# A fused attention and gated feed-forward kernel: tile 3 of batch 0 moved into tile 1's gates, three tiles of batch 1 transposed by DMA, numerators and loads of batches 2 and 3 rescheduled

## The chip, the cores and the metric

The kernel runs on one core of one Trainium2 chip. The metric is device time in microseconds (us), and lower is better. Besides the timed runs there is one profiled execution, of which the trace holds the start and the length of every instruction and every DMA packet. The engines are named as the profile names them: PE is TensorE (PEld its weight loads), DVE is VectorE, ACT is ScalarE, POOL is GpSimd and SP is SyncE, which in this kernel only issues DMAs.

## The reference: what is computed

A linear attention ("cosFormer") over 8 batches, 8 heads, 576 positions and a head size of 64 is followed by a gated feed-forward layer with RMS normalization. All inputs and outputs are float32.

```python
def phi(x, c, s):                       # c, s: cos and sin of pi/2 * pos / S
    r = np.maximum(x, 0.0)
    return np.concatenate([r * c, r * s], axis=-1)      # 128 features
q_p, k_p = phi(q, cos_w, sin_w), phi(k, cos_w, sin_w)
kv  = np.einsum('bhsf,bhsd->bhfd', k_p, v)
z   = np.sum(k_p, axis=2)
num = np.einsum('bhsf,bhfd->bhsd', q_p, kv)
den = np.einsum('bhsf,bhf->bhs', q_p, z)[..., None] + 1e-06
x   = (num / den).transpose(0, 2, 1, 3).reshape(B * S, H * D)   # 4608 x 512
xn  = x / sqrt(mean(x * x) + 1e-6) * rms_g
g   = xn @ w_gate                                       # 512 -> 1536
out = (silu(g) * (xn @ w_val)) @ w_out                  # 1536 -> 512
```

## The kernel before, in words

**Tiles and blocks.** The 576 positions of a batch are split into four tiles of 128 (j = 0 to 3) and a tail of 64. Two tails make one tail tile of 128 rows, so there are four of those. The feed-forward layer works on blocks of 512 rows: blocks 0 to 7 are the four tiles of batches 0 to 7, and block 8 is the four tail tiles. Blocks are worked in the order 0, 1, 2, 3, 4, 5, 6, 8, 7.

**The steps of one tile.** `q_phi` makes the features of q (tile `qp`) on DVE and ACT, a transposition turns them (`q_tr_pe` on PE or `q_tr_dma` by DMA) into `qpT`. `nd_pe` (L418; matmuls at L421) multiplies them with the batch's key-value product and gives numerators and denominators of eight heads in the one PSUM tile `psA`. `nd_post` (L479) reads `psA` on DVE: an addition (L461), a reciprocal (L464) and a product (L471), which leaves the tile's x in SBUF. `x_sq` (L483) takes the mean square on ACT and the power -1/2 on POOL; `x_norm` (L495, DVE L499) gives the normalized tile `xn` in bf16. The next `nd_pe` can write `psA` only when the product L471 of the one before has read it.

**The transposition of a normalized tile.** The gate and value matmuls need the tile transposed in `xnT`. On PE this is `x_tr_pe` (four 128x128 transpositions, L518) into a PSUM bank, and `x_tr_evac` (L520) copies the bank to `xnT` on ACT or DVE. By DMA it is `x_tr_dma` (L511, one instruction on SP's queue, L512).

**The key-value product.** `k_phi` makes key features, `v_cast` casts v, and `kvz_pe` sums over positions into `psA`. A batch's k, v and q are loaded to tiles `raw`, of which there are five in a ring (`load_kv`, `load_q`); `load_q_tails` loads the tails of two batches. Batches up to 2 have k and v in one layout, batches from 3 on in a "wide" layout (`wide(b)`), whose load is one DMA of 112 rows and one or two small ones. Loads go through SP's queue or through POOL's.

**One feed-forward block.** For each of 12 chunks n, `gval_mm` (L528) makes four gate matmuls into `psG[n % 2]` and four value matmuls into `psV[n % 2]`; `gval_h` takes the SiLU on ACT (L547) and the product on DVE (L548) into `hT`. Two banks of each kind alternate. Then `out_step` (L551) makes 12 matmuls for each of four output tiles into `psC[j % 2]`, and `out_store` copies and stores them.

**The order is written by hand.** The schedule is manual: each engine runs its instructions in the order of the program and waits by semaphores. `at(blk, n, where, f, ...)` puts a call in a slot of a block: `gval_step` runs the slot's "pe" list, then the matmuls of chunk n, then the "pre" list, then SiLU and product, then the "post" list. Slots 12 to 15 are the four output steps, which have a "mid" as well. `out_first` is the output of block 0: 48 matmuls in the order of its list `todo`, 12 of them to a slot, with slots 12 to 15 around them.

**Block 0 starts by hand.** Before the slots there is straight-line code (L578 to L709) for batch 0. Its first chunks are worked in units: `units[i] = (j0, j1, n0, n1)` are the tiles and chunks of unit i. Units 0 to 3 are one tile wide (tiles 0, 1, 0, 1; chunks 0 to 3, then 4 to 7), units 4 to 7 are tiles 2 and 3 together with two chunks each. `unit_mm(i, wg)` writes `psG[i % 2]`, `unit_mm(i, wv)` writes `psV[i % 2]`, `unit_silu(i)` and `unit_h(i)` follow. `filler(n, bank)` is n matmuls of zeros. The core of what the change touches there reads:

```python
    unit_mm(3, wg)                 # tile 1, chunks 4-7
    x_tr_pe(0, 3, psC[0])          # tile 3 transposed
    x_tr_evac(V, 0, 3, psC[0])
    unit_silu(3)
    unit_h(1)
    unit_mm(4, wg)                 # tiles 2 and 3, chunks 0-1
    for i in range(2, 4):
        unit_mm(i, wv)
        unit_h(i)
    unit_silu(4)
```

**Batch 1 and batch 2 around the change.** The list `X1` (L744) places the four tiles of batch 1 within `out_first`: `nd_pe`, `nd_post` and `x_sq` of tile j at the first place, `x_norm` at the second, the transposition on PE (`x_tr`) at the third. Batch 2's tiles have `nd_pe` in chunks 6, 8, 10 and 12 of block 1 and `x_norm` with `x_tr_dma` one slot later. Batch 2's q is loaded by POOL's queue in slot 11 of block 0, batch 3's k, v and q by SP's queue in slots 0, 5 and 8 of block 1.

Of the kernel before, what the change touches and what calls it, by code (L numbers as in the profile page):

```python
# [17 lines left out]
def kernel(  # L18
# [11 lines left out]
    nc = tc.nc  # L30
    B, H, S, D = q.shape
    DM = H * D
    DFF = moe_w_gate.shape[1]
    P = 128
    TB = 512
    HP = H // 2
# [4 lines left out]
    NDT = DM // P  # L41
# [5 lines left out]
    V, A, G = nc.vector, nc.scalar, nc.gpsimd  # L47
# [10 lines left out]
    psG = [ps.tile([P, 512], FP32, name=f"psG{i}") for i in range(2)]  # L58
    psV = [ps.tile([P, 512], FP32, name=f"psV{i}") for i in range(2)]
    psC = [ps.tile([P, 512], FP32, name=f"psC{i}") for i in range(2)]  # L60
# [13 lines left out]
    def wide(b):  # L74
        return b > 2
# [4 lines left out]
    def kv_rows5(src, b, r0, r1):  # L80
        part = src[b, :, 0 : NC5 * (KP - 1), :].rearrange(
            "h (p c) d -> p h (c d)", c=NC5
        )[r0 : min(r1, KP - 1)]
        return bass.AP(part.tensor, part.offset, [[NC5 * D, r1 - r0]] + list(part.ap)[1:])
# [6 lines left out]
    def raw_tile(which, b):  # L91
        if (which, b) not in raw:
            t = ring.tile([P, H * NC5 * D], FP32, name="raw", tag="raw")
            raw[(which, b)] = t
        return raw[(which, b)]

    def raw_kv(which, b):
        t = raw_tile(which, b)
        if wide(b):
            return t[:, :].rearrange("p (h e) -> p h e", h=H)  # L100
        return t[:, 0 : HP * NC * D].rearrange("p (hp e) -> p hp e", hp=HP)
# [4 lines left out]
    def load_kv(which, b, hps=(0, HP), eng=nc.sync):  # L106
        src = k if which == "k" else v
        if not wide(b):
            return eng.dma_start(
                out=raw_kv(which, b)[:, hps[0] : hps[1], :], in_=kv_rows(src, b, hps)  # L110
            )
        last = KP if b < B - 1 else KP - 1
        for r0, r1 in ((0, KM), (KM, last)):
            eng.dma_start(out=raw_kv(which, b)[r0:r1, :, :], in_=kv_rows5(src, b, r0, r1))
        if last < KP:
            eng.dma_start(
                out=raw_kv(which, b)[last:KP, :, :].rearrange("p h (c d) -> p h c d", d=D),
                in_=src[b, :, S - 1 : S, :].rearrange("h s d -> s h d").unsqueeze(2)
                .to_broadcast([1, H, NC5, D]),
            )  # L120
# [19 lines left out]
    for c0, c1 in ((0, 4), (4, NC)):  # L140
        nc.sync.dma_start(
            out=raw_kv("k", 0)[:, :, c0 * D : c1 * D],
            in_=kv_rows(k, 0, (0, HP))[:, :, c0 * D : c1 * D],
# [24 lines left out]
    wg = one.tile([P, NDT, DFF], BF16, name="wg")  # L168
    wv = one.tile([P, NDT, DFF], BF16, name="wv")
# [42 lines left out]
    part, left = [], 1e-6  # L212
# [8 lines left out]
    def g_spread(bank, t):  # L221
# [12 lines left out]
        out=th[:, 0:NTAB], in0=fidx[:, :], scalar1=S - 1.0, scalar2=ang,  # L234
        op0=ALU.min, op1=ALU.mult,
    )
    for c0, c1, less in ((0, 9, 576.0), (13, 14, 64.0)):
        V.tensor_scalar(
            out=th[64:128, c0:c1], in0=fidx[64:128, c0:c1], scalar1=-less, scalar2=ang,
# [3 lines left out]
        out=th[:, NTAB : 2 * NTAB], in0=th[:, 0:NTAB], scalar1=math.pi / 2.0,  # L243
# [4 lines left out]
        out=sel[:, :, :], in_=ident[0:4, 0:4].unsqueeze(2).to_broadcast([4, NDT, P])  # L248
# [17 lines left out]
    xnT = [one.tile([P, NDT, TB], BF16, name=f"xnT{i}") for i in range(2)]  # L266
# [212 lines left out]
    def nd_post(b, j):  # L479
        nd_rec(b, j)  # L480
        nd_div(b, j)
# [38 lines left out]
    def x_tr_evac(eng, b, j, bank, ts=(0, NDT)):  # L520
        dst = bank.bitcast(BF16).rearrange("p (t s) -> p t s", s=P)
        copy(eng, x_dst(b, j)[:, ts[0] : ts[1], :], dst[:, ts[0] : ts[1], :])
# [48 lines left out]
    def filler(n, bank):  # L571
        for _ in range(n):
            nc.tensor.matmul(
                bank[:, :], lhsT=warm[:, 0:P], rhs=warm[:, :], start=True, stop=True
            )
# [30 lines left out]
    units = [(j, j + 1, 4 * i, 4 * i + 4) for i in range(2) for j in range(2)]  # L606
    units += [(2, 4, n, n + 2) for n in range(0, 8, 2)]
    sg_of = {}

    def unit_mm(i, w, by_rows=False):  # L610
        j0, j1, n0, n1 = units[i]
        bank = (psG if w is wg else psV)[i % 2]
        width = (j1 - j0) * P
        todo = [(n, t) for n in range(n0, n1) for t in range(NDT)]
        if by_rows:
            todo = [(n, t) for t in range(NDT) for n in range(n0, n1)]
        for n, t in todo:
            nc.tensor.matmul(  # L618
                bank[:, (n - n0) * width : (n - n0 + 1) * width],
                lhsT=w[:, t, n * P : (n + 1) * P],  # L620
                rhs=xnT[0][:, t, j0 * P : j1 * P],
                start=(t == 0 and (n == n0 or not by_rows)),
                stop=(t == NDT - 1 and (n == n1 - 1 or not by_rows)),
                skip_group_check=by_rows,
            )

    def unit_silu(i):
        sg_of[i] = four.tile([P, TB], FP32, name="sg", tag="sg")
        A.activation(out=sg_of[i][:, :], in_=psG[i % 2][:, 0:TB], func=AF.Silu)

    def unit_h(i):
        j0, j1, n0, n1 = units[i]
        V.tensor_tensor(
            out=hT[:, n0:n1, j0 * P : j1 * P],
            in0=psV[i % 2][:, 0:TB].rearrange("p (n s) -> p n s", n=n1 - n0),
            in1=sg_of[i][:, :].rearrange("p (n s) -> p n s", n=n1 - n0), op=ALU.mult,
        )
# [32 lines left out]
    q_tr_evac(A, 0, 3, qbank[3])  # L670
    x_norm(0, 1)
    nd_post(0, 2)
    filler(2, psG[1])
    unit_mm(0, wg, by_rows=True)
    x_tr_pe(0, 1, psC[0])
    x_tr_evac(V, 0, 1, psC[0])
# [16 lines left out]
    x_tr_evac(V, 0, 2, psC[1])  # L693
    unit_silu(2)
    unit_h(0)
    unit_mm(3, wg)
    x_tr_pe(0, 3, psC[0])
    x_tr_evac(V, 0, 3, psC[0])
    unit_silu(3)
    unit_h(1)  # L700
    unit_mm(4, wg)
    for i in range(2, 4):
        unit_mm(i, wv)
        unit_h(i)
    unit_silu(4)
    unit_mm(5, wg)
    unit_mm(4, wv)
    unit_silu(5)
# [4 lines left out]
    def at(blk, n, where, f, *args):  # L713
        slots.setdefault((blk, n), {}).setdefault(where, []).append((f, args))
# [19 lines left out]
    at(0, 10, "post", load_kv, "v", 2, (0, HP), G)  # L734
    at(0, 12, "pe", kvz_pe, 1)
    at(0, 12, "pe", kvz_evac, A, 1)
    at(0, 11, "post", load_q, 2, (0, 4), G)

    def x_tr(b, j, bank):
        x_tr_pe(b, j, bank)  # L740
# [3 lines left out]
    X1 = (  # L744
        ((12, "mid"), (13, "pe"), (14, "pe")),
        ((13, "pe"), (13, "mid"), (14, "mid")),
        ((13, "mid"), (14, "pe"), (15, "pe")),
        ((14, "pe"), (14, "mid"), (15, "mid")),
    )
# [3 lines left out]
        if j:  # L753
            at(0, *X1[j - 1][1], x_norm, 1, j - 1)
    at(0, *X1[3][1], x_norm, 1, 3)
    for j in range(4):
        at(0, *X1[j][2], x_tr, 1, j, psV[j % 2])
    for nb in range(2, B):
        b = nb - 1
        first = nb == 2  # L760
        for i, cs in enumerate(KCS5 if wide(nb) else KCS):
            kb, kn = ((0, 14), (0, 15), (1, 0), (1, 1))[i] if first else (b - 1, 12 + i)
            for c in cs:
                at(kb, kn, "post", k_phi, V, nb, c, 0)
                at(kb, kn, "post", k_phi, A, nb, c, 1)
        for i in range(2):
            vb, vn = ((0, 15), (1, 0))[i] if first else (b - 1, 13 + 2 * i)
            at(vb, vn, "post", v_cast, V, nb, (2 * i, 2 * i + 2))
        for j in range(4):
            qb, qn = (b, 1 + j) if first else ((b - 1, 14), (b - 1, 15), (b, 0), (b, 1))[j]  # L770
            at(qb, qn, "post", q_phi, V, nb, j, 0)
            at(qb, qn, "post", q_phi, A, nb, j, 1)
            at(qb, qn, "post", q_tr_dma, nb, j)
        kz = 3 if first else 2
        at(b, kz, "pe", kvz_pe, nb)
        at(b, kz, "pre", kvz_evac, A, nb)
        for j in range(4):
            n = ((6, 8, 10, 12) if first else (4, 6, 8, 10))[j]
            at(b, n, "pe", nd_pe, nb, j)
            at(b, n, "pre", nd_post, nb, j)  # L780
            at(b, n, "post", x_sq, nb, j)
            at(b, n + 1, "post", x_norm, nb, j)
            at(b, n + 1, "post", x_tr_dma, nb, j)

    for pair in range(4):
        b = 2 * pair or 3
        if pair == 0:
            at(1, 15, "post", load_q_tails, 0)
        at(b, 3, "post", q_tails_phi, V, pair, 0)
        at(b, 3, "post", q_tails_phi, A, pair, 1)  # L790
        at(b, 3, "post", q_tails_tr_dma, pair)
        at(b, 12, "pe", nd_tails_pe, pair)
        at(b, 12, "pre", nd_post, 2 * pair + 1, 4)
        at(b, 12, "post", x_sq, 2 * pair + 1, 4)
        at(b, 13, "post", x_norm, 2 * pair + 1, 4)
        at(b, 13, "post", x_tr_dma, 2 * pair + 1, 4)
    for nb in range(3, B):
        b = nb - 2
        late = b == 1
        at(b, 0, "post", load_kv, "k", nb)  # L800
        at(b, 5 if late else 3, "post", load_kv, "v", nb)
        at(b, 8 if late else 6, "post", load_q, nb)
        if nb % 2 == 1:
            at(b, 9, "post", load_q_tails, nb // 2)

    def gval_step(blk, n):
        run(blk, n, "pe")
# [86 lines left out]
```

## Time and profile before

| What | Value |
|---|---|
| Runs | 324.9, 325.15 and 326.33 us; median 325.15 us |
| The profiled execution | 324.66 us, of which the span from first to last instruction is 322.9 us |
| Granted TensorE clock over the span | 0.999 |
| Mean DMA rate | 165 GB/s; 53.37 MB in 77627 packets |
| Matmuls of the feed-forward layer, spacing in a chunk | four in 0.86 us |
| Start of block 1's first gate matmul | 55.80 us |
| Start of block 2's first gate matmul | 89.22 us |

The profiled execution lies 0.49 us below the median of the runs and 0.24 us below the lowest of them, and its span is 1.76 us shorter than its own time. Times of single instructions are given from the start of the span. A duration of a matmul row is longer than its share of the pipeline: a row of four that "took" 1.03 us is followed by the next row 0.86 us after its start, so costs on PE are read from start to start.

### The profile page before, as it was taken

The numbers are of one execution on the slowest core, as the hardware profiler recorded it, in microseconds if no ns is written. First come the engines' busy times: TensorE is split into PE (matmuls) and PEld (weight loads), VectorE is DVE, ScalarE is ACT, GpSimd is POOL, SyncE is SP. The second block draws the span as 40 slices with busy tenths as digits, with TensorE's granted clock in tenths as the row PEclk, the third lists the DMA queues.
The fourth block names the chain that finished last, engine by engine and source line by source line (L and its number), as shares of the span: only waits on it lengthen the run. The fifth ranks groups of instructions, "written<-read, shape, count | busy, mean of one in ns | idle before, by whom it ended". The sixth has DMA issues, their size and how long they took to land.

```text
span 322.9 us, 6078 instructions
## 1 busy us (share of the span) xinstructions
PE 315.6 (98%) x2312; PEld 163.5 (51%) x2348; DVE 185.5 (57%) x380; ACT 164.9 (51%) x319; POOL 40.6 (13%) x78
## 2 busy tenths in 40 slices
PE   8999999999999999999999999999999999999996
PEld 3688565544454445444544445444544444444444
DVE  8875958767636773676457745781577034204410
ACT  5664766744665457445754575446644333223321
POOL 9771302001001100011001000110011000000000
PEclk9999999999999999999999999999999999999999
DMA  7999996999789966998699959994822300041002
GB/s 229 233 266 272 283 327 240 230 200 240 149 156 232 234 190 161 195 233 202 175 198 214 210 148 207 202 217 141 119 49 48 117 32 0 2 98 31 3 32 97
DMA packets 77627, 53.37 MB, mean 165 GB/s; under 512 B 50410, under 2 KB 71326, under 8 KB 77598
## 3 DMA queue, kind: packets, MB, share of 16 engines
q1 hardware_dynamic: 70374, 39.81, 58.2%
q0 software_dynamic: 7216, 13.17, 16.5%
q8 instruction: 18, 0.29, 0.4%
q14 instruction: 11, 0.09, 0.1%
q10 hardware_dynamic: 8, 0.00, 0.0%
HBM read 37.83 MB, written 9.44 MB: 146 GB/s over the span
## 4 chain that ended last, share of the span: by engine, by line
PE 93%; DMA 2%; DVE 2%; issue 1%; POOL 0%; ACT 0%; ACTq 0%; POOLq 0%
PE psV L528 27%; PE psC L551 27%; PE psG L528 26%; PE psA L421 2%; DMA raw<-in_q_dram 2%; PE psG L551 2%; PE psV L618 2%; PE psA L359 2%; PE psG L618 1%; PE psA L366 1%; DVE xn L499 1%; PE psV L335 0%; PE psA L446 0%; DVE xt L471 0%; PE psG L402 0%
## 5 line engine op out<-in xcount | busy, mean ns | idle before, releaser
L548 DVE TENSOR_TENSOR hT<-psV,sg 128x512 bf16<-128x512 f32 x100 | 68.9, 689 | 102.1 <-PE psV L528 65.0
L547 ACT ACTIVATE sg<-psG 128x512 f32<-128x512 f32 x100 | 59.2, 592 | 62.5 <-PE psG L528 54.6
L528 PE MATMUL psV<-xnT,wv 128*128 128x512 bf16 x345 | 89.8, 379 | 0.6
L528 PE MATMUL psG<-xnT,wg 128*128 128x512 bf16 x338 | 88.6, 379 | 0.6 <-issue 0.2
L551 PE MATMUL psC<-wo,hT 128*128 128x512 bf16 (+1 forms) x398 | 88.6, 376 | 0.5
L551 PEld LDWEIGHTS <-hT 128*128 128x128 bf16 x456 | 42.9, 98 | 47.1
L528 PEld LDWEIGHTS <-wv 128*128 128x128 bf16 x400 | 39.1, 98 | 47.2
L528 PEld LDWEIGHTS <-wg 128*128 128x128 bf16 x400 | 37.0, 98 | 39.8
L492 POOL TENSOR_TENSOR rs<-ms,mhalf 128x1 f32<-128x1 f32 x36 | 19.8, 550 | 195.6 <-ACT scr L487 195.6
L275 ACT COPY osb<-psC 128x512 f32<-128x512 f32 x32 | 18.7, 585 | 50.0 <-PE psC L551 46.1
L487 ACT ACTIVATE scr<-xt 128x513 bf16<-128x513 f32 x36 | 22.8, 635 | 25.2 <-DVE xt L471 25.1
L499 DVE SCALAR_TENSOR_TENSOR xn<-xt,rs,gb 128x512 bf16<-128x512 f32 (+1 forms) x37 | 26.9, 730 | 10.3 <-POOL rs L492 10.3
L281 ACT ACTIVATE kp<-raw,tab 128x256 bf16<-128x256 f32 (+2 forms) x51 | 28.8, 607 | 2.3 <-DMA raw<-in_k_dram 2.3
L471 DVE TENSOR_TENSOR xt<-psA,rec 128x512 f32<-128x512 f32 x36 | 24.9, 692 | 1.2
L281 ACT ACTIVATE qp<-raw,tab 128x512 bf16<-128x512 f32 x32 | 22.6, 714 | 0.8 <-DMA raw<-in_q_dram 0.8
L283 DVE TENSOR_SCALAR kp<-raw,tab 128x256 bf16<-128x256 f32 (+2 forms) x53 | 20.4, 429 | 0.3 <-DMA raw<-in_k_dram 0.3
L283 DVE TENSOR_SCALAR qp<-raw,tab 128x512 bf16<-128x512 f32 x31 | 15.5, 506 | 0.3 <-DMA raw<-in_q_dram 0.3
L421 PEld LDWEIGHTS <-qpT 128*128 128x128 bf16 x224 | 10.5, 97 | 6.6 <-issue 0.5
L528 PE MATMUL psV<-xnT_tail,wv 128*128 128x512 bf16 x48 | 12.3, 379 | 0.1
L528 PE MATMUL psG<-xnT_tail,wg 128*128 128x512 bf16 x46 | 12.1, 379 | 0.1
L421 PE MATMUL psA<-kvzs,qpT 128*128 128x65 bf16 x224 | 11.4, 193 | 0.0
L277 DVE CAST vv<-raw 116x1280 bf16<-116x1280 f32 (+1 forms) x13 | 10.5, 807 | 0.0
(97 smaller groups left out, 181.2 us busy)
## 6 DMA issues: line engine op xcount, KB each, us to landing
out_dram<-osb SPq DMA_DIRECT2D x31, 256.0 KB, 2.4
raw<-in_k_dram SPq DMA_DIRECT2D x5, 1120.0 KB, 8.4
raw<-in_v_dram SPq DMA_DIRECT2D x5, 1120.0 KB, 8.5
raw<-in_q_dram SPq DMA_DIRECT2D x5, 1024.0 KB, 8.9
raw<-in_k_dram POOLq DMA_DIRECT2D x2, 1152.0 KB, 19.4
raw<-in_v_dram POOLq DMA_DIRECT2D x2, 1152.0 KB, 16.1
raw<-in_q_dram POOLq DMA_DIRECT2D x2, 1024.0 KB, 16.1
wg<-in_moe_w_gate_dram POOLq DMA_DIRECT2D x3, 512.0 KB, 14.2
```

Of the source, the lines that this page charges most:

```text
L275: A.copy(out=o, in_=i)
L281: A.activation(out=out_ap, in_=in_ap, func=AF.Relu, scale=scale)
L283: eng.tensor_scalar(out=out_ap, in0=in_ap, scalar1=scale, scalar2=0.0, op0=ALU.mult, op1=ALU.max)
L421: nc.tensor.matmul(heads[:, g, hp, :], lhsT=qpT[:, h, j * P : (j + 1) * P], rhs=kvzs[b][:, g, hp * E : (hp + 1) * E], start=True, stop=True,)
L471: V.tensor_tensor(out=xt[:, 0:DM].rearrange("p (hp g d) -> p g hp d", g=2, d=D), in0=heads[:, :, :, 0:D], in1=rec[:, :, :].unsqueeze(3).to ...
L487: A.activation(out=scr[:, :], in_=xt[:, 0 : DM + 1], func=AF.Square, scale=1.0 / math.sqrt(DM), accum_out=ms[:, :],)
L492: G.tensor_tensor(out=rs[:, :], in0=ms[:, :], in1=mhalf[:, :], op=ALU.pow)
L499: V.scalar_tensor_tensor(out=xn_of[(b, j)][:, c], in0=x_of[(b, j)][:, c], scalar=rs_of[(b, j)][:, :], in1=gb[:, c], op0=ALU.mult, op1=ALU. ...
L528: nc.tensor.matmul(bank[:, cols[0] : cols[1]], lhsT=w[:, t, n * P : (n + 1) * P], rhs=x[:, t, cols[0] : cols[1]], start=(t == 0), stop=(t ...
L547: A.activation(out=sg[:, :], in_=g[:, 0:TB], func=AF.Silu)
L548: V.tensor_tensor(out=hT[:, n, :], in0=v[:, 0:TB], in1=sg[:, :], op=ALU.mult)
L551: nc.tensor.matmul(bank[:, 0 : cols[1] - cols[0]], lhsT=hT[:, n, j * P : (j + 1) * P], rhs=wo[:, n, cols[0] : cols[1]], start=(n == 0), st ...
```

## The change

- In the units of block 0, the gate matmuls of unit 3 are split: 12 matmuls, then the transposition of tile 3, then the other four. The copy of tile 3 goes from DVE to ACT. Unit 4's gate matmuls, eight of 256 columns, become two groups of eight of 128 columns (`unit_tile`): tile 2's right away, tile 3's after the value matmuls of unit 2. One of two filler matmuls before unit 0 goes.
- Tiles 0, 1 and 2 of batch 1 are transposed by DMA, each issued in the slot of its `x_norm`, and only tile 3 by PE. Batch 2's q is loaded by SP's queue in slot 14 "mid" of block 0, behind those three, where POOL's queue had it in slot 11.
- Batch 2's third and fourth `nd_pe` move from chunks 10 and 12 of block 1 to 9 and 11, and with them what follows.
- Batch 3's k, v and q are loaded in slots 4, 7 and 12 of block 1 (0, 5 and 8 before), its `q_phi` and `q_tr_dma` come one slot later, and the tails are loaded in other slots: pair 0 in block 2, slot 9 (block 1, slot 15 before), pair 1 in block 1, slot 13 (slot 9 before); the other pairs stay.
- For batches 4 to 7 the large DMA of v is split in two halves of the heads.

```diff
@@ load_kv
         last = KP if b < B - 1 else KP - 1
+        parts = ((0, H),) if which == "k" or b == 3 else ((0, HP), (HP, H))
         for r0, r1 in ((0, KM), (KM, last)):
-            eng.dma_start(out=raw_kv(which, b)[r0:r1, :, :], in_=kv_rows5(src, b, r0, r1))
+            for h0, h1 in parts if r0 == 0 else ((0, H),):
+                eng.dma_start(
+                    out=raw_kv(which, b)[r0:r1, h0:h1, :],
+                    in_=kv_rows5(src, b, r0, r1)[:, h0:h1, :],
+                )
@@ unit_mm
-    def unit_mm(i, w, by_rows=False):
+    def unit_mm(i, w, by_rows=False, part=(0, 16)):
...
-        for n, t in todo:
+        for n, t in todo[part[0] : part[1]]:
...
+    def unit_tile(i, j):
+        j0, j1, n0, n1 = units[i]
+        for n in range(n0, n1):
+            c = ((n - n0) * (j1 - j0) + j - j0) * P
+            for t in range(NDT):
+                nc.tensor.matmul(
+                    psG[i % 2][:, c : c + P], lhsT=wg[:, t, n * P : (n + 1) * P],
+                    rhs=xnT[0][:, t, j * P : (j + 1) * P],
+                    start=(t == 0), stop=(t == NDT - 1),
+                )
@@ block 0 by hand
-    filler(2, psG[1])
+    filler(1, psG[1])
     unit_mm(0, wg, by_rows=True)
...
-    unit_mm(3, wg)
+    unit_mm(3, wg, part=(0, 12))
     x_tr_pe(0, 3, psC[0])
-    x_tr_evac(V, 0, 3, psC[0])
+    x_tr_evac(A, 0, 3, psC[0])
+    unit_mm(3, wg, part=(12, 16))
     unit_silu(3)
     unit_h(1)
-    unit_mm(4, wg)
-    for i in range(2, 4):
-        unit_mm(i, wv)
-        unit_h(i)
+    unit_tile(4, 2)
+    unit_mm(2, wv)
+    unit_h(2)
+    unit_tile(4, 3)
     unit_silu(4)
+    unit_mm(3, wv)
+    unit_h(3)
     unit_mm(5, wg)
@@ slots
-    at(0, 11, "post", load_q, 2, (0, 4), G)
...
-    for j in range(4):
-        at(0, *X1[j][2], x_tr, 1, j, psV[j % 2])
+    for j in range(3):
+        at(0, *X1[j][1], x_tr_dma, 1, j)
+    at(0, *X1[3][2], x_tr, 1, 3, psV[1])
+    at(0, *X1[3][1], load_q, 2)
...
-            qb, qn = (b, 1 + j) if first else ((b - 1, 14), (b - 1, 15), (b, 0), (b, 1))[j]
+            late = j + (nb == 3)
+            qb, qn = (b, 1 + j) if first else (b - (late < 2), (14 + late) % 16)
...
-            n = ((6, 8, 10, 12) if first else (4, 6, 8, 10))[j]
+            n = ((6, 8, 9, 11) if first else (4, 6, 8, 10))[j]
...
-        if pair == 0:
-            at(1, 15, "post", load_q_tails, 0)
+        at(*((2, 9), (1, 13), (3, 9), (5, 9))[pair], "post", load_q_tails, pair)
...
-        late = b == 1
-        at(b, 0, "post", load_kv, "k", nb)
-        at(b, 5 if late else 3, "post", load_kv, "v", nb)
-        at(b, 8 if late else 6, "post", load_q, nb)
-        if nb % 2 == 1:
-            at(b, 9, "post", load_q_tails, nb // 2)
+        for which, n in zip("kvq", (4, 7, 12) if b == 1 else (0, 3, 6)):
+            if which == "q":
+                at(b, n, "post", load_q, nb)
+            else:
+                at(b, n, "post", load_kv, which, nb)
```

## The prediction

> **What bounds the kernel.** I read the page's head first, then PE's waits, then PE's timeline from 0 to 130 us, and last DVE and SP around each edit.
>
> ```profile
> span 322.9 us, 6078 instructions
> ...
> PE 315.6 (98%) x2312; PEld 163.5 (51%) x2348; DVE 185.5 (57%) x380; ACT 164.9 (51%) x319; POOL 40.6 (13%) x78
> ...
> PEclk9999999999999999999999999999999999999999
> ```
>
> PE is busy 98% at the full clock, so only two things can move the end: work taken from PE, and waits of PE that go or come. The view of PE's waits shows that hardly any are left after the first microseconds:
>
> ```profile
> PE psC L573 <- DVE warm L154: 1.2, 1, 1.2
> PE psG L618 <- DVE xnT L277: 0.5, 1, 0.5
> ```
>
> Columns: total wait, times, longest. From 55.80 us, block 1, to 89.22 us, block 2, are 33.42 us. 144 matmuls at 0.86/4 us are 31.0, batch 2's `kvz_pe` with its pauses is 1.4 and four `nd_pe` at 0.245 are 1.0, so block 1 has nothing to give: any wait made there is a loss.
>
> **Part 1, tile 3 among tile 1's gates: 0.70 us gained.** PE's timeline (start, duration, engine, line, operation, count):
>
> ```profile
> 22.67 1.06 PE L618 MATMUL psG<-xnT,wg 128*128 128x128 bf16 x16
> 23.56 0.39 PE L518 MATMUL psC<-ident,xn 128*128 128x128 bf16 x4
> 24.48 1.05 PE L618 MATMUL psG<-xnT,wg 128*128 128x256 bf16 x8 [0.53 <-DVE xnT L277]
> 25.36 1.95 PE L618 MATMUL psV<-xnT,wv 128*128 128x128 bf16 x32
> 27.15 1.04 PE L618 MATMUL psG<-xnT,wg 128*128 128x256 bf16 x8
> ```
>
> The transposition at 23.56 takes 0.22 (as at 22.45 to 22.67) and ends its share at 23.78; unit 4 starts at 24.48. The 0.70 between is the wait for DVE's copy (24.01 to 24.42, behind unit 0's product). After: 12 matmuls of 0.0555 from 22.67, transposition at 23.34 (its `xn` is ready at 22.41 + 0.75 = 23.16), four matmuls from 23.56, tile 2's eight from 23.78, unit 2's values from 24.22, tile 3's eight from 25.11, unit 3's values from 25.55, unit 5 at 26.44 against 27.15. Sixteen matmuls of 128 columns cost 0.89, eight of 256 cost 0.88, so the split costs 0.01. Each cover holds: ACT copies tile 3 from about 23.79 to 24.36 (0.57 as for batch 1), wanted at 25.11; if this cover went, PE would wait as before. `psV[0]` is read by unit 0's product until 24.09, wanted at 24.22. The value weights of chunks 4 to 7 are issued at 7.53 and land 16.0 later, at 23.5, also in time. ACT's SiLU of unit 3 moves behind the copy, to about 24.9, and unit 5 wants its bank at 26.44. What is then late next would be data: the output weights' second part lands at 22.33 + 20.0 = 42.3, wanted at 43.74 - 0.70 = 43.0; q of batch 1 lands at 34.5, which ACT meets 0.3 late, PE not at all. So 0.70 stands until block 1.
>
> **Part 2, the filler: 0.02.** One filler is 0.216 us. Behind unit 0's gates PE needs tile 1's `xn` (DVE 17.52 + 0.75 = 18.27; PE's transposition starts at 18.35), and after it the first value weights (issued 6.07, landing 12.4 later, 18.5; matmul at 18.58). PE would just wait 0.2 earlier. Bounds 0 to 0.22; I take 0.02, the distance that the row leaves. The clock stays full over such a pause (the 0.53 at 24 us left it at 1.00).
>
> **Part 3, three transpositions off PE: 0.65 gained, about 0.1 lost.**
>
> ```profile
> 49.73 0.38 PE L518 MATMUL psV<-ident,xn 128*128 128x128 bf16 x4
> 49.95 1.46 PE L551 MATMUL psC<-wo,hT 128*128 128x512 bf16 x6
> ...
> 54.28 0.39 PE L518 MATMUL psV<-ident,xn 128*128 128x128 bf16 x4
> 54.50 1.46 PE L551 MATMUL psC<-wo,hT 128*128 128x512 bf16 x5
> 55.80 1.03 PE L528 MATMUL psG<-xnT,wg 128*128 128x512 bf16 x4
> ```
>
> Each costs 49.95 - 49.73 = 0.22; three are 0.65. Block 1 would start at 55.80 - 0.70 - 0.65 = 54.45 (0.02 less with part 2). Tile 3 is turned at 54.28 - 1.35 = 52.93, its `xn` ready at 53.38 - 0.70 = 52.68. Its copy on DVE stands behind three `k_phi` and an output copy: `xn` to 52.68, `k_phi` to 53.5, output copy to 54.1, copy to 54.4, so up to 0.1 late. Tile 2's DMA is issued when `xn` is ready, 51.05 + 0.74 - 0.70 = 51.1. How long does it take? SP's transposes in 237 to 249 us, with nothing beside them:
>
> ```profile
> L512 SPq DMA_TRANSPOSE xnT<-xn x4: 1191/1192/1192, 237.3 to 248.5; - x4
> ...
> DMA to landing us min/median/max: 2.5/2.5/2.5
> ```
>
> That gives 53.6, 0.8 ahead. The other bound is the median of all 24 on the page, 7.8, which gives 58.9 and a wait of 4.5; those stand behind megabyte loads on SP's own queue. Here SP's queue holds only the two earlier tiles, but POOL's still carries v of batch 2 (issued 38.6, landing 13.1 later, 51.7) while q, 49 to 54 us, has left it. I take 2.5 to 3.3 and 0.1 for both copies together, range 0 to 4.5. Behind the transposes SP issues q and the output stores. [...] ACT wants it at 59.88 - 1.3 = 58.6. [...] I cost it at 0.
>
> [...]
>
> **Part 4, batch 2's third numerators in chunk 9: 0.74 lost.** PE and DVE around chunk 8 of block 1, as now:
>
> ```profile
> 71.22 0.41 PE L421 MATMUL psA<-kvzs,qpT 128*128 128x65 bf16 x8
> 71.49 0.69 DVE L548 TENSOR_TENSOR hT<-psV,sg 128x512 bf16<-128x512 f32 x1 [1.04 <-PE psV L528]
> 72.10 0.74 DVE L499 SCALAR_TENSOR_TENSOR xn<-xt,rs,gb 128x512 bf16<-128x512 f32 x1
> 72.76 0.16 DVE L461 TENSOR_SCALAR rec<-psA 128x8 f32<-128x8 f32 x1
> ...
> 73.19 0.69 DVE L471 TENSOR_TENSOR xt<-psA,rec 128x512 f32<-128x512 f32 x1
> 73.19 1.03 PE L528 MATMUL psG<-xnT,wg 128*128 128x512 bf16 x4
> ```
>
> Chunk 7's product and tile 0's `x_norm` stand on DVE ahead of tile 1's `nd_post`, which reads `psA` until 73.88. PE reaches chunk 9 at 73.19, and `nd_pe` of tile 2 now stands there. It writes `psA`, so PE waits until 73.88 and about 0.06 (24.42 to 24.48 above): 73.94, a wait of 0.75. All of chunk 9 is queued behind it. Bounds: 0.75, or 0 if DVE were ahead, but all its steps start from PE's own chunk 7 and nothing in the edit shortens them; I take 0.74. The fourth, in chunk 11, finds `psA` long free.
>
> **Part 5, loads and features: 0.** Tile 3 of batch 2 goes out two to three microseconds earlier than at 85.29, where it already had slack to 89.22. q of batch 3 goes out near 84 instead of 74.19 and lands near 89; DVE's first q feature waits for it, ahead of block 2's first product, which now comes at 91.75 and is wanted by PE only at chunk 2, near 94. The k and v of batch 3 leave SP's queue free for batch 2's features. SP's extra instruction per split v is 0.5 us on a queue that PE doesn't wait for. Bounds 0 to 1 (a late feature in block 2).
>
> **Sum.** -0.70 - 0.02 - 0.65 + 0.10 + 0.74 = -0.53. Against the profiled execution, 324.66, that is 324.1; against the median of the runs, 325.15, it is 324.6, which I predict.
>
> **Rivals.** (a) The numerators' wait does not appear: -1.27, 323.9. For it: only that the wait rests on DVE's order being what I read. Against: the same pair in block 0 waits already (PE's `nd_pe` at 47.79, DVE's product ends at 47.73). (b) Slower: tile 2's transposition lands late at the start of block 1, because it shares engines with v of batch 2. At the median 7.8 the wait is 4.5 in place of 0.1 and the time 329.0; it decides from a landing 3.9 us after issue, where the wait eats the 0.53 and the kernel is not faster any more; over 0.5% slower needs 5.5 us. For it: DMA is busy through 48 to 52 us. Against: 52 to 54 is nearly idle. (c) Part 1 does nothing, because ACT's copy or the weights come late: -0.53 + 0.70 = +0.17, 325.3. Against: margins of 0.7.
>
> **How the numbers follow.** 0.5%, 1.6 us, is about what a measurement of this kernel tells from no change. Forecast 0.70 (its own range 324.0 to 325.2); (a) 0.10; (b) 0.15, of which 0.10 beyond 326.8; (c) 0.05. All but part of (b) and the edge of (a) lie within 0.5%: faster 0.06, same 0.83, slower 0.11. The range takes in (a), (c) and the smaller half of (b): 323.6 to 326.3.
>
> **What would show it.** Right: no wait of PE at 24 us and unit 5's gates at 26.4; block 1 at 54.4 to 54.7; a wait of PE for DVE's product L471 of about 0.75 before chunk 9 of block 1; block 2 at 88.6. Wrong: PE waiting for a DMA at 54 us, or no wait at chunk 9.

## The result, and the profile after

The changed kernel is slower by a little: 325.59 us median (325.02 to 326.23) against 325.02 us (324.61 to 326.33), 22 runs each, ratio 1.0016 with a 95% interval of 1.0010 to 1.0023. The forecast was 0.5 us faster. Forecast and result both lie within the 0.5% that the prediction takes for no change, but the sign is wrong: some 1.1 us went another way than the sum had it. Two runs, one of 476 us in experiment 7 and one of 1898 us of the kernel before beside it, are left out of the ratios below.

The profiled execution took 325.34 us with a span of 323.5, 0.6 us more than before. PE is as busy as before (315.5 us, 98% of the span), at a granted clock of 1.00. The view of PE's waits (total, times, longest, all above 0.5 us) has two new lines in place of the one that the change was to remove:

```profile
PE psC L578 <- DVE warm L159: 1.2, 1, 1.2
PE psA L426 <- DMA qpT<-qp: 1.1, 1, 1.1
PE psA L426 <- DVE xt L476: 0.6, 1, 0.6
```

(Lines of the changed kernel are five higher than those of before, from the loads to the units; L638 is the new `unit_tile`.) PE's timeline of the changed kernel tells where each stands; the columns are as before, start and duration first:

```profile
23.55 0.39 PE L623 MATMUL psG<-xnT,wg 128*128 128x128 bf16 x4
23.77 0.61 PE L638 MATMUL psG<-xnT,wg 128*128 128x128 bf16 x8
...
26.45 1.04 PE L623 MATMUL psG<-xnT,wg 128*128 128x256 bf16 x8
...
54.46 1.04 PE L533 MATMUL psG<-xnT,wg 128*128 128x512 bf16 x4
```

```profile
71.00 1.03 PE L533 MATMUL psV<-xnT,wv 128*128 128x512 bf16 x4
72.61 0.40 PE L426 MATMUL psA<-kvzs,qpT 128*128 128x65 bf16 x8 [0.58 <-DVE xt L476]
...
88.63 1.03 PE L533 MATMUL psG<-xnT,wg 128*128 128x512 bf16 x4
...
103.31 1.03 PE L533 MATMUL psV<-xnT,wv 128*128 128x512 bf16 x4
105.46 0.42 PE L426 MATMUL psA<-kvzs,qpT 128*128 128x65 bf16 x8 [1.12 <-DMA qpT<-qp]
...
123.70 1.03 PE L533 MATMUL psG<-xnT,wg 128*128 128x512 bf16 x4
```

Read as a ledger against the kernel before: unit 5's gates at 26.45 (27.15 before, -0.70), block 1 at 54.46 (55.80, -1.34), block 2 at 88.63 (89.22, -0.59: the wait at 71.86 took 0.75 back), block 3 at 123.70 (122.98, +0.72). So up to block 2 the forecast held within 0.1 us, and the whole miss is one wait in block 2: the numerators of batch 3's third tile, due when the matmuls from 103.31 end at 104.17, started at 105.46. It waited 1.29 us for a transposition of q features by DMA. The chain of waits follows that transposition back to its issue (start, duration, what):

```profile
95.21 0.64 PE psG L533 x3
95.85 9.57 DMA qpT<-qp
105.41 0.05 issue
105.46 0.42 PE psA L426 x8
```

9.57 us from issue to landing, where the median of this size was 3.8 us before. What stands ahead of it is seen in SP's timeline, first of the kernel before, then of the changed one:

```profile
94.02 1.25 SPq L318 DMA_TRANSPOSE qpT<-qp  x1
95.37 1.35 SPq L114 DMA_DIRECT2D raw<-in_k_dram  x2
96.88 1.26 SPq L318 DMA_TRANSPOSE qpT<-qp  x1
```

```profile
91.49 2.99 SPq L323 DMA_TRANSPOSE qpT<-qp  x2
94.58 1.11 SPq L116 DMA_DIRECT2D raw<-in_k_dram  x2
95.85 6.71 SPq L323 DMA_TRANSPOSE qpT<-qp  x2
```

Before, three of batch 3's four feature transpositions were issued ahead of batch 4's k (1.1 MB) and one behind it. After, with the features one slot later, two are ahead and two behind. The fourth had time until chunk 10; the third is wanted in chunk 8.

### The profile page after: what moved, and what is told of

It reads as the page before. It is cut to its first block, busy times and chain, and to the rows that moved or that the text cites. A ratio compares the mean times of both kernels' runs of the same rounds, so it can differ in the third digit from the quotient of the medians.

```text
span 323.5 us, 6075 instructions
## 1 busy us (share of the span) xinstructions
PE 315.5 (98%) x2307; PEld 162.6 (50%) x2343; DVE 184.6 (57%) x378; ACT 164.8 (51%) x318; POOL 39.9 (12%) x77
## 4 chain that ended last, share of the span: by engine, by line
PE 89%; DMA 7%; POOL 2%; issue 1%; DVE 1%; POOLq 0%; DVEq 0%
PE psC L556 27%; PE psV L533 25%; PE psG L533 25%; DMA wv<-in_moe_w_val_dram 4%; DMA qpT<-qp 3%; PE psV L623 2%; PE psA L426 2%; PE psG L556 2%; PE psA L364 2%; PE psG L623 2%; PE psA L371 1%; POOL raw L128 1%; PE psA L451 0%; POOL vv L208 0%; PE psC L340 0%
## 5 line engine op out<-in xcount | busy, mean ns | idle before, releaser
L504 DVE SCALAR_TENSOR_TENSOR xn<-xt,rs,gb 128x512 bf16<-128x512 f32 (+1 forms) x37 | 26.9, 731 | 9.9 <-POOL rs L497 9.9
L288 DVE TENSOR_SCALAR qp<-raw,tab 128x512 bf16<-128x512 f32 x31 | 14.7, 479 | 6.4 <-DMA raw<-in_q_dram 6.4
```

The source lines that it names most:

```text
L288: eng.tensor_scalar(out=out_ap, in0=in_ap, scalar1=scale, scalar2=0.0, op0=ALU.mult, op1=ALU.max)
L504: V.scalar_tensor_tensor(out=xn_of[(b, j)][:, c], in0=x_of[(b, j)][:, c], scalar=rs_of[(b, j)][:, :], in1=gb[:, c], op0=ALU.mult, op1=ALU. ...
```

## The experiments

Two theories were set against each other. **Q (the queue):** the third transposition is late because batch 4's k now stands ahead of it on SP's queue. **L (the late q):** it is late because batch 3's q, loaded in slot 12, lands late (DVE's first q feature waited 6.1 us for it) and everything after it is late. All timed runs had five rounds, each beside runs of the kernel before on the same chip; ratios are to those.

**1. k of batch 4 behind the transpositions.**

```diff
-        for which, n in zip("kvq", (4, 7, 12) if b == 1 else (0, 3, 6)):
+        for which, n in zip("kvq", (4, 7, 12) if b == 1 else (2, 3, 6) if b == 2 else (0, 3, 6)):
```

> The changed kernel with one edit: k of batch 4 is loaded in slot 2 of block 2 in place of slot 0, so that its megabyte stands behind batch 3's third and fourth feature transpositions on SP's queue, not ahead of them. Theory Q (the queue: the third transposition waits behind that megabyte): PE's wait before chunk 8 of block 2 (1.12 us in the profile, 1.29 us from start to start) is gone, the third transposition lands about 3 us after its issue, block 3 starts 1.2 to 1.3 us earlier, and the time is 324.2 to 324.5, ratio to the kernel before 0.997 to 0.9985. Theory L (the late q: batch 3's q, loaded in slot 12, lands at 90.1 and everything after it is late): the wait stays at 0.8 us or more and the time within 0.4 us of the changed kernel's 325.6. New cost to look for: batch 4's k features in slot 12 of block 2 waiting for k.

Measured: 324.1 us, ratio 0.9980 (0.9971 to 0.9988). SP's timeline of this run has the four together and k behind; PE's waits keep only the one of block 1, and block 3 starts at 122.48 against 123.70:

```profile
91.86 5.99 SPq L323 DMA_TRANSPOSE qpT<-qp  x4
97.96 1.08 SPq L116 DMA_DIRECT2D raw<-in_k_dram  x2
```

```profile
PE psC L578 <- DVE warm L159: 1.2, 1, 1.2
PE psA L426 <- DVE xt L476: 0.6, 1, 0.6
```

Q holds: moving one load behind two transpositions turns the change from slower to faster. The first of the four is issued no earlier than in the changed kernel (91.86 against 91.49), so q was as late. The third took 5.4 us from issue (94.99) to landing (100.41), more than the 3 expected, but it was there 3.8 us before PE wanted it at 104.25.

**2. Only batch 3's q earlier.** Slot 8 in place of 12.

```diff
-        for which, n in zip("kvq", (4, 7, 12) if b == 1 else (0, 3, 6)):
+        for which, n in zip("kvq", (4, 7, 8) if b == 1 else (0, 3, 6)):
```

> The changed kernel with one edit: q of batch 3 is loaded in slot 8 of block 1 as before the change, not in slot 12; features stay one slot later. Theory Q: q lands before 86, the features are made about 1 us earlier, but the third transposition is still issued behind k of batch 4, so a wait of 0.3 us or more before chunk 8 of block 2 stays; time 324.6 to 325.6. Theory L: the wait is gone, time 324.2 to 324.5. Side effect under both: the x transpositions of batch 2 stand behind q, without a wait of PE at block 2's start.

Measured: 325.41 us, ratio 1.0017 (1.0008 to 1.0026), and 0.98 us of wait for `qpT` left of 1.12. The first feature transposition was issued 0.6 us earlier (90.88), k at 93.95 and the third behind it at 95.18. L falls: an earlier q alone gains nothing.

**3. Features back as well.** As 2, with batch 3's features in the slots of before.

```diff
-            late = j + (nb == 3)
+            late = j
```

> a2_q3_early (q of batch 3 loaded in slot 8) with batch 3's features and their transpositions back in the slots of before, one earlier. The third transposition is then issued ahead of k of batch 4, only the fourth behind it, as before the change. Theory Q: the wait before chunk 8 of block 2 goes, 324.1 to 324.4, ratio to the kernel before 0.997 to 0.9985. If it were not the order against k of batch 4 that decides, a wait of 0.5 us or more stays as in a2 (325.4).

Measured: ratio 0.9989 (0.9979 to 0.9998), median 324.71. The profiled execution, 324.12 us, is as expected and has no wait in block 2; the median is 0.3 above what was expected, and its runs spread from 323.96 to 324.95. What the others wait for was not profiled. Against run 2 the third transposition has its place ahead of k, but it also goes out 2.7 us earlier (92.51 against 95.18), so these two runs do not separate order from lateness as experiment 1 does (94.99 against 95.85). The run's own trace is the better evidence for Q: the third, ahead of k, landed 3.2 us after its issue (95.68), and the fourth, issued at 95.07 directly behind k, took 10.3 us (105.35), in time for chunk 10. The gain is smaller than in run 1.

**4. Numerators back in chunks 10 and 12.** The change moved them to 9 and 11, at a price of 0.75.

```diff
-            n = ((6, 8, 9, 11) if first else (4, 6, 8, 10))[j]
+            n = ((6, 8, 10, 12) if first else (4, 6, 8, 10))[j]
```

> The changed kernel with batch 2's third and fourth numerators back in chunks 10 and 12 of block 1. PE's wait for DVE's product before chunk 9 (0.58 us in the profile, 0.75 from start to start) is gone and block 2 starts about 0.7 us earlier, near 87.9. The wait in block 2 stays and may grow, because q of batch 3 now goes out behind a later transposition: 1.1 to 2.0. Time 324.8 to 325.6. If the 0.75 were only moved, block 2 would start at 88.6 as in the changed kernel.

Measured: 326.19 us, ratio 1.0045 (1.0024 to 1.0065). A miss: in the profiled execution (327.56 us) the wait in block 1 did go, but a larger one came at the start of block 2, 2.12 us for `xnT`. The expectation had q of batch 3 go out behind a later transposition; it goes out ahead of it. With both edits, this and k behind:

> Both edits: k of batch 4 behind the transpositions, numerators back in chunks 10 and 12. Theory Q: both waits are gone, 0.75 and 1.29 us from the changed kernel's 325.6, so 323.5 to 323.8, ratio to the kernel before 0.995 to 0.997. Theory L: only 0.75 goes and the other wait grows, 324.8 to 325.6.

Measured: 325.84 us, ratio 1.0037 (1.0021 to 1.0053), also a miss, for the same reason. SP's timeline of this run, and its chain of waits at the start of block 2:

```profile
81.58 0.39 SPq L128 DMA_DIRECT2D raw<-in_q_dram  x1
83.71 0.35 SPq L567 DMA_DIRECT2D out_dram<-osb  x1
84.15 1.26 SPq L517 DMA_TRANSPOSE xnT<-xn  x1
```

```profile
84.15 5.87 DMA xnT<-xn
90.03 0.04 issue
90.07 1.02 PE psG L533 x4
```

Tile 3's x transposition moves to slot 13 with its numerators, and q of batch 3, a megabyte loaded in slot 12, is now ahead of it: 5.87 us from issue to landing, where it took 3.3 in the changed kernel (82.14 to 85.42) and 2.4 in the kernel before, and PE waits 1.83 us. This is mechanism Q a second time, at another place. The chunks of the numerators are all that differs from experiment 1, so this also shows what the step to chunk 11 does: with q in slot 12, the fourth numerators must be done by then.

**5. The same with q one slot later still, slot 13.**

```diff
-        for which, n in zip("kvq", (4, 7, 12) if b == 1 else (2, 3, 6) if b == 2 else (0, 3, 6)):
+        for which, n in zip("kvq", (4, 7, 13) if b == 1 else (2, 3, 6) if b == 2 else (0, 3, 6)):
```

> As a4_k4_nd (numerators back in chunks 10 and 12, k of batch 4 behind), but q of batch 3 one slot later still, slot 13 of block 1, so behind tile 3's x transposition. Theory Q: a4 lost its gain because q's megabyte stood ahead of that transposition; then PE's wait for xnT at block 2's start (1.83 us) goes, and the time is 323.4 to 324.2 unless the still later q (landing near 92) makes a new wait of numerators in chunk 4 of block 2. If numerators in 10 and 12 are slow for another reason, the wait at block 2's start stays and the time is above 325.

Measured: 327.24 us, ratio 1.0075 (1.0050 to 1.0100). The wait for `xnT` is gone, as Q has it, but the late q now makes a wait of its own, earlier than expected: not of the numerators, but of ACT. ACT waits 5.83 us for q, until 96.24, with block 2's SiLU queued behind the q features, so that PE lacks a bank. In the profiled execution, which at 330.75 us is 3.5 above the median, PE's wait is:

```profile
PE psG L533 <- ACT sg L552: 3.6, 1, 3.6
```

So theory L has a place too: slot 13 is too late for q.

**6. The wait in block 1.** Run 1's kernel, with `x_norm` and the x transposition of batch 2's tile 0 in slot 8 in place of 7.

```diff
-            at(b, n + 1, "post", x_norm, nb, j)
-            at(b, n + 1, "post", x_tr_dma, nb, j)
+            m = n + 2 if first and j == 0 else n + 1
+            at(b, m, "post", x_norm, nb, j)
+            at(b, m, "post", x_tr_dma, nb, j)
```

> The changed kernel with k of batch 4 behind the transpositions (as in a1_k4_behind) and with x_norm and the x transposition of batch 2's tile 0 moved one slot later, from 7 to 8, so that on DVE tile 1's nd_post no longer stands behind that x_norm (0.74 us). If the wait before chunk 9 of block 1 is DVE's order, as the prediction's part 4 has it, it shrinks from 0.75 to about 0.1 us and the time is 323.4 to 323.7, ratio to the kernel before 0.995 to 0.9965. If the wait has another cause, the time stays at a1's 324.1.

Measured: 323.58 us, ratio 0.9954 (0.9938 to 0.9970). The view of PE's waits has nothing over 0.2 us after the first microseconds. DVE's timeline around chunk 8 of block 1 shows why; the changed kernel first, then this one:

```profile
70.17 0.69 DVE L553 TENSOR_TENSOR hT<-psV,sg 128x512 bf16<-128x512 f32 x1 [1.03 <-PE psV L533]
70.78 0.74 DVE L504 SCALAR_TENSOR_TENSOR xn<-xt,rs,gb 128x512 bf16<-128x512 f32 x1
...
71.87 0.69 DVE L476 TENSOR_TENSOR xt<-psA,rec 128x512 f32<-128x512 f32 x1
```

```profile
70.17 0.69 DVE L553 TENSOR_TENSOR hT<-psV,sg 128x512 bf16<-128x512 f32 x1 [1.03 <-PE psV L533]
70.78 0.16 DVE L466 TENSOR_SCALAR rec<-psA 128x8 f32<-128x8 f32 x1
...
71.21 0.69 DVE L476 TENSOR_TENSOR xt<-psA,rec 128x512 f32<-128x512 f32 x1
```

Without the 0.74 us of `x_norm` (L504) ahead of it, the product that frees `psA` ends at 71.90 in place of 72.56, and chunk 9, due at 71.86, hardly waits. This is the version that beats both kernels, by 1.5 us against the one before (0.0046 of 325).

**7. Parts alone, on the kernel before.** Tile 3 amid tile 1's gates, which is the whole of the change to the units (`part`, `unit_tile`, the copy on ACT) and no more:

```diff
-    unit_mm(3, wg)
+    unit_mm(3, wg, part=(0, 12))
     x_tr_pe(0, 3, psC[0])
-    x_tr_evac(V, 0, 3, psC[0])
+    x_tr_evac(A, 0, 3, psC[0])
+    unit_mm(3, wg, part=(12, 16))
...
```

> The kernel before with part 1 alone (tile 3 amid tile 1's gates, two fillers as before). Prediction's part 1: no wait of PE for xnT at 24 us, everything up to block 1 is 0.70 us earlier, and the rest follows: 324.2 to 324.4, ratio 0.9975 to 0.9985. Rival: the gain is eaten before the end by loads that don't move with PE, ratio 0.999 to 1.001.

Measured: 324.4 us, ratio 0.9978 (0.9966 to 0.9991), 0.7 us: part 1 is worth what it was priced at, and keeps it to the end. The three DMA transpositions with q of batch 2 on SP's queue, and nothing else moved:

```diff
-    at(0, 11, "post", load_q, 2, (0, 4), G)
...
-    for j in range(4):
-        at(0, *X1[j][2], x_tr, 1, j, psV[j % 2])
+    for j in range(3):
+        at(0, *X1[j][1], x_tr_dma, 1, j)
+    at(0, *X1[3][2], x_tr, 1, 3, psV[1])
+    at(0, *X1[3][1], load_q, 2)
```

> The kernel before with the DMA transposition of three tiles of batch 1 and q of batch 2 on SP's queue alone; k of batch 3 stays in slot 0 of block 1. Block 1 starts about 0.6 us earlier. Then k of batch 3 (1.1 MB) stands directly behind q and ahead of batch 2's feature transpositions, which by theory Q land 1 to 3 us later than before: a wait of PE for qpT at chunk 6 of block 1 between 0 and 1.5 us, time 324.4 to 326.0. Without such a wait 324.4 to 324.6.

Measured: 329.61 us, ratio 1.0126 (1.0087 to 1.0165), far over the range. The wait was expected and in its place, but three times the size:

```profile
PE psA L421 <- DMA qpT<-qp: 4.4, 1, 4.4
```

The first feature transposition of batch 2, issued at 60.90 behind q and k, landed 10.72 us later. In the changed kernel, which has k in slot 4 in place of 0, it was issued at 60.03, landed 4.8 us later, and no such wait is left. So the DMA transpositions need a later k of batch 3; a run with that load alone moved was not made.

**8. The small piece first.** In the changed kernel the transpositions behind k of batch 4 go slowly. The run asks whether the order of k's two pieces has a part in it. Packets of transpositions (256 bytes each) that started in each microsecond, from the trace:

```
from us          94   95   96   97   98   99  100  101  102  103  104  105
changed kernel  851  607    0    0    0    0  226  260  321  371  312 1031
k behind (1)    543  803  721  313  598   18  500    0    0    0  173  283
```

```diff
-        for r0, r1 in ((0, KM), (KM, last)):
+        for r0, r1 in ((KM, last), (0, KM)):
```

> The changed kernel with the order of a wide load's two pieces turned round: the 4-row piece (40 KB) is issued before the 112-row piece. In the changed kernel the transpositions behind k of batch 4 crawl at about 300 packets in a microsecond for five microseconds, where they elsewhere go at about 1000. [...]

Measured: 325.19 us, ratio 0.9998 (0.9987 to 1.0008). The wait for `qpT` was 0.43 us in the profiled execution against 1.12 in the changed kernel, but the transposition did not land sooner:

```profile
95.67 9.71 DMA qpT<-qp
105.39 0.05 issue
105.43 0.42 PE psA L426 x8
```

It took 9.71 us against 9.57, and chunk 8's numerators start at 105.43 against 105.46. The wait is shorter because PE came later: a wait of 0.83 us for q features near 10 us had put block 2 at 89.30 in place of 88.63. Block 3 starts at 123.67 against 123.70. So this trace shows no gain from the order of the pieces; why the median is 0.4 us lower than the changed kernel's was not profiled. Why the transpositions crawl at 300 packets a microsecond for five microseconds is open.

**9. The filler and the split of v undone.**

```diff
-        parts = ((0, H),) if which == "k" or b == 3 else ((0, HP), (HP, H))
+        parts = ((0, H),)
...
-    filler(1, psG[1])
+    filler(2, psG[1])
```

> The changed kernel with the second filler matmul back before unit 0 and v of batches 4 to 7 loaded in one large DMA as before. The prediction costs both at next to nothing (0.02 and 0): the same two waits in blocks 1 and 2, time within 0.3 us of the changed kernel's 325.6, ratio to the kernel before 1.0005 to 1.0025. If either mattered, the time would leave that range.

Measured: 325.73 us, ratio 1.0028 (1.0016 to 1.0039), with both waits in place (0.6 and 1.3 us). The ratio is a little over the expected range, but its interval overlaps that of the changed kernel, so the two together can't be told from nothing. Each alone was not run.

## Why the prediction was right and wrong, by its own steps

**Part 1, 0.70 gained: right.** Unit 5's gates were put at 26.44 and came at 26.45; alone the part gave a ratio of 0.9978. Rival (c) falls.

**Part 2, the filler, 0.02: right as far as runs can tell.** In the changed kernel unit 0's gates start at 17.03 (17.46 before), and the first value matmuls at 18.55 against 18.58. The page's chain names the value weights' DMA there, 4% of the span.

**Part 3, 0.65 gained and 0.1 lost: right.** Block 1 was put at 54.4 to 54.7 and came at 54.46. The last of the three transpositions was issued at 51.30 and landed at 53.77, 2.5 us later; the two before it, issued at 47.72 and 49.42 while POOL's queue still carried v (landed 51.33), took 4.2 and 3.1. Of the two bounds weighed there, 2.5 and 7.8 us, the last transposition kept to the lower. That q of batch 2 costs 0 was the author's estimate; in the changed kernel it was issued at 52.69 and landed at 59.1, 0.5 later than ACT wanted it by the step, and ACT waited 0.48 us for it, PE not at all. Rival (b), a late transposition at block 1, did not come.

**Part 4, 0.74 lost: right,** 0.75 from start to start, and experiment 6 shows the cause named: DVE's order. Rival (a) falls.

**Part 5, loads and features at 0: wrong, and the whole of the miss.** The step reads "Bounds 0 to 1 (a late feature in block 2)", and took 0. It followed q of batch 3 to DVE's and ACT's first feature and found cover there, which the runs bear out: ACT and DVE did wait for q (0.70 and 6.1 us), and PE did not. But it did not follow the features on to their transpositions. One slot later puts the third one behind batch 4's k on SP's queue, a load that the change does not touch and that the step did not name. The step calls this "a queue that PE doesn't wait for"; PE waited for it. A transposition behind a megabyte cost 9.57 us there, and the numerators of chunk 8 had 8.3 us of room (95.85 to 104.17). Size of the miss: 1.29 us in place of 0, above the bound of 1. Rows of the kernel before would have shown the danger and not the full price: part 3 reads 7.8 us as the median of transpositions behind megabyte loads, and batch 3's fourth, behind this very k, took 7.7 (96.88 to 104.54). At either price the third would have landed 0.5 to 0.7 us in time.

**The sum.** Of the -0.53 forecast, -0.59 was there at block 2's start; +1.29 turned it to +0.72 at block 3 and to +0.6 in the span and in the medians.

## What to carry to other kernels

Here a transposition by DMA landed late where a load stood ahead of it on its queue: 9.57 us after its issue behind k in the changed kernel, against 3.2 ahead of k in experiment 3. When a step moves by a slot, list what it passes on the queue, also the loads that stay where they are, and price it at the landing seen behind such a load, not at the one seen alone. Moves in a tuned schedule belong together; here q in slot 12 needed the numerators in chunk 11, and the DMA transpositions a later k of batch 3. Where a step is brought closer, look at the other engine's order: one instruction of 0.74 us, put behind the one that frees the bank, was worth as much as part 1.

## What the runs showed of the hardware

In these runs PE's waits of 2.12 us and more cost more than themselves. Windows over the run of experiment 7 with the DMA transpositions alone (us of the stretch; its length; busy time of PE, PEld, DVE, ACT and POOL; granted clock; DMA share; GB/s):

```profile
66.00:71.60 5.60, 1.23 (x6) 0.39 (x4) 1.39 (x3) 0.60 (x1) 0.00 (x0) 0.99 1.34 123
71.60:75.00 3.40, 3.33 (x16) 1.49 (x17) 1.06 (x3) 0.97 (x2) 0.00 (x0) 0.52 1.07 202
75.00:80.00 5.00, 4.95 (x31) 2.40 (x31) 3.45 (x7) 1.74 (x5) 0.55 (x1) 1.00 0.87 232
```

After 4.4 us without matmuls the granted clock was 0.52 for 3.4 us: four matmuls of 512 columns took 1.70 us from start to start (72.09 to 73.79) in place of 0.86. The waits of 3.64 us (experiment 5) and 2.12 us (first run of experiment 4) were followed by means of 0.60 and 0.67; after 1.83 us (second run of experiment 4) and after the 1.12 us of the changed kernel it was 1.00. So the clock was halved after the longest wait, and a wait of 2.12 us was enough in one run to bring its mean down to 0.67 over the 3.6 us that followed.
